# A six-layer cross network on one core: how the first rows come in and the last rows go out

## The chip, the core and the metric

The kernel runs on one core of a Trainium2 chip. TensorE (PE) multiplies matrices and writes PSUM. VectorE (DVE) and ScalarE (ACT) read PSUM and write on-chip memory (SBUF), GpSimd (POOL) computes on SBUF alone, and SyncE (SP) issues transfers. Transfers (DMAs) are issued from the queues of SP, ACT and POOL. The metric is the device time of one execution in microseconds (us). The profile's span is the part of it between the first and the last recorded instruction.

## The reference

```python
B, F, D, L = 4096, 26, 16, 6          # Din = F * D = 416
x = x0                                # (4096, 416), bf16
for l in range(L):                    # ws: (6, 416, 416), bs: (6, 416)
    x = x0 * (x @ ws[l] + bs[l]) + x
```

Written out, x stays x0 times a sum, so the kernel keeps the sum in PSUM: after layer l, PSUM holds the sum over all layers so far of x_l @ ws[l], the bias is the running sum of bs, and x_(l+1) = x0 * (PSUM + bias sum), where that bias sum begins with a one.

## The kernel before

**Layout.** x0 and x are kept transposed: features on partitions, rows along the free dimension. The 416 features are three chunks of 128 (`NC = 3`) and a rest of 32 that is called the tail. The 4096 rows are four super-blocks of 1024 rows (`SB`), each with two halves of 512 (`H`), half A and half B. For each super-block the six layers run one after the other, so there are 24 periods of the same shape.

**One period.** TensorE multiplies half A's three chunks (`chunk(m, 0)`), then the tail's rows (`row`, line 351, and the matmul at line 367), then the tail's columns, then half B's three chunks. All matmuls of weights are cut in tiles of 32 columns (`tile_mm`, line 212), four of which run side by side. VectorE turns each finished PSUM bank into the next x (`scalar_tensor_tensor`, line 459). ScalarE, GpSimd and again ScalarE do the same for the tail (lines 506, 199, 486).

**The start.** The first 768 rows of x0 come as plain rows into `xin_sb`, whose slot j holds rows 128j to 128j+127; TensorE transposes them. Only rows 768 to 1023 and the later super-blocks are transposed by the DMA itself. Line 121 (SP) loads slots 0 and 1, line 474 (ACT) slots 2 and 3, each in one transfer of 208 KB; line 123 loads slots 4 and 5. Between them stand layer 0's weights (`w_sb`, lines 122 and 475), and on ACT the tail's last rows (`xtl_sb`) and two of the four pieces of layer 0's tail weights (`load_wt`, line 107; the two others are issued by POOL). TensorE first multiplies constants (`fill(14)`: 14 rounds of four matmuls with 256 columns), whose result is thrown away, then makes twelve 128x128 transposes (line 250) in the order of `IN_ORDER`, pairs (h, c) of 256-row half and chunk. VectorE copies chunks 0 and 2 of each to `x0T_sb` (line 432), ScalarE chunk 1 (line 481). Layer 0 of half A then runs with k outermost: for each k, it waits for that chunk's copies and multiplies it with all three output chunks. Before k = 2 come the bias sums, the transposes of the tail and those of slots 4 and 5.

**The end.** The last super-block's output is transposed back by TensorE into PSUM and copied to `o_sb`, whose slots are again 128 rows. Half A's chunks are transposed between the matmuls of the last layer and copied by ScalarE (line 527). Half B (slots j0+4 to j0+7) follows at the end: eight transposes of chunks 0 and 1 into PSUM bank 4, then four of chunk 2 into banks 5 and 0 (line 406), and three copies out: VectorE copies chunks 0 and 1 of all four slots in one instruction (line 464), ScalarE chunk 2 of slots j0+4 and j0+5 (line 537), VectorE chunk 2 of slots j0+6 and j0+7 (line 468). SP stores slots j0+6 and j0+7 (line 159), ACT slots j0+4 and j0+5 (line 543).

**Order.** Every engine's program is written out by hand, and each engine runs its own in order; semaphores tie them together. A wait holds back all that stands behind it on the same engine, DMA issues too. `s_xin[h]` counts landed loads of half h, 16 for each transfer; `s_inT` the finished transposes, two at a time; `s_inD` and `s_inA` the copies by VectorE and ScalarE; `s_pB` the output transposes; `s_oeD`, `s_oeA` and `s_oet` the output copies.

Of the kernel before, what the change touches and what calls it, by code (L numbers as in the profile page):

```python
# [8 lines left out]
ACTF = mybir.ActivationFunctionType  # L9


def bass_standalone__dcn_v2_cross__recsys_kernel(
# [8 lines left out]
    NC = 3  # L21
    DF = 128 * NC
# [8 lines left out]
    NL = NS * L  # L31

    with ExitStack() as es:  # L33
# [8 lines left out]
        xin_sb = sb("xin_sb", [128, 6, D])  # L42
# [11 lines left out]
        o_sb = sb("o_sb", [128, NJ, D])  # L54
# [6 lines left out]
        psT = ps.bitcast(BF16)  # L61
# [7 lines left out]
        s_xin = [sem("s_xin%d" % i) for i in range(3)]  # L69
        s_xtl0, s_x4 = sem("s_xtl0"), [sem("s_x4%d" % i) for i in range(NS - 1)]  # L70
        s_w = [sem("s_w%d" % i) for i in range(L)]
        s_wt = [sem("s_wt%d" % i) for i in range(2)]
        s_x0T = [sem("s_x0T%d" % i) for i in range(NS)]
        s_inT, s_inD, s_inA = sem("s_inT"), sem("s_inD"), sem("s_inA")
        s_tp, s_te = sem("s_tp"), sem("s_te")
        s_ti, s_to, s_mb = sem("s_ti"), sem("s_to"), sem("s_mb")
        s_xa, s_xb = sem("s_xa"), sem("s_xb")
# [3 lines left out]
        s_pA, s_pB, s_pt, s_out = sem("s_pA"), sem("s_pB"), sem("s_pt"), sem("s_out")  # L81
        s_oet, s_oeA, s_oeD = sem("s_oet"), sem("s_oeA"), sem("s_oeD")

        x0_v = x0.rearrange("(j p) d -> p j d", p=128)
# [7 lines left out]


        IN_BANKS = ((3, 4, 6), (0, 5, 7))
        IN_ORDER = ((0, 0), (1, 0), (0, 1), (1, 1), (0, 2), (1, 2))
        THIRD = (3, 6, 7)
        HALVES = (slice(0, 64), slice(64, 128))

# [6 lines left out]
        def load_wt(eng, g, a, b, done):  # L105
            n0, n1 = ((0, 256), (256, DF))[g % 2]
            eng.dma_start(
                wt_sb[lane(g), a:b, 0:n1 - n0], ws[a:b, DF:D, n0:n1].rearrange("l p n -> p l n")
            ).then_inc(done, 16)

        @block.sync
        def _(sp):
            def load_rows(s):
                sp.dma_start_transpose(
                    x4_sb[:, s - 1:s, :], x0[s * SB:(s + 1) * SB, D - 128:D]
                ).then_inc(s_x4[s - 1], 16)
                sp.dma_start_transpose(
                    x0T_sb[:, :, s * SB:(s + 1) * SB], x0[s * SB:(s + 1) * SB, 0:DF]
                ).then_inc(s_x0T[s], 16)

            sp.dma_start(xin_sb[:, 0:2, :], x0_v[:, 0:2, :]).then_inc(s_xin[0], 16)
            sp.dma_start(w_sb[:, 0, 0, :], ws[0, 0:128, :]).then_inc(s_w0, 16)
            sp.dma_start(xin_sb[:, 4:6, :], x0_v[:, 4:6, :]).then_inc(s_xin[2], 16)
            sp.dma_start_transpose(x0T_sb[:, :, 768:SB], x0[768:SB, 0:DF]).then_inc(s_x0T[0], 16)
            for l in range(1, L):
                if l > 1:
                    sp.wait_ge(s_ti, (1, 2, 2, 2)[l - 2])
                if l == L - 1:
                    load_rows(1)
                sp.dma_start(w_sb[:, l, :, :], wmain(l)).then_inc(s_w[l], 16)  # L130
                if l == 1:
                    for g in range(4):
                        load_wt(sp, g, 1, L, s_wt[1])
            for s in range(NS - 1):
                n = (s + 1) * L
                sp.wait_ge(s_xa, NC * n)
                sp.wait_ge(s_xb, NC * n)
                for c in range(NC):
                    sp.dma_start_transpose(
                        o_sb[:, s * JS:(s + 1) * JS, c * 128:(c + 1) * 128], xo_sb[:, s, c, :]  # L140
                    ).then_inc(s_oT, 16)
                sp.wait_ge(s_xt, n)
                sp.dma_start_transpose(ot_sb[:, s, :, :], xot_sb[:, s, :]).then_inc(s_ot, 16)
                if s < NS - 2:
                    load_rows(s + 2)
                sp.wait_ge(s_oT, 16 * NC * (s + 1))
                sp.wait_ge(s_otc, s + 1)
                sp.dma_start(
                    out_v[:, s * JS:(s + 1) * JS, :], o_sb[:, s * JS:(s + 1) * JS, :]
                ).then_inc(s_out, 16)  # L150
            j = (NS - 1) * JS
            sp.wait_ge(s_oeA, 2)
            sp.dma_start(out_v[:, j:j + 4, 0:256], o_sb[:, j:j + 4, 0:256]).then_inc(s_out, 16)
            sp.wait_ge(s_oeA, 3)
            sp.wait_ge(s_oet, 1)
            sp.dma_start(out_v[:, j:j + 4, 256:D], o_sb[:, j:j + 4, 256:D]).then_inc(s_out, 16)
            sp.wait_ge(s_oeD, 2)
            sp.wait_ge(s_oet, 1)
            sp.dma_start(out_v[:, j + 6:j + 8, :], o_sb[:, j + 6:j + 8, :]).then_inc(s_out, 16)
            sp.wait_ge(s_out, 16 * (NS + 3))  # L160
# [49 lines left out]
        def _(pe):  # L210
# [8 lines left out]
            def fill(n):  # L219
                for i in range(n):  # L220
                    for q in range(4):
                        tile_mm(ps[lane(q), 7, 0:256], const[:, 0:32], const, q, True)
# [18 lines left out]
                            )  # L241
                    ins.then_inc(s_inT, 1)

            fill(14)
            pe.wait_ge(s_set, 1)
            for i, (h, c) in enumerate(IN_ORDER):
                if i in (0, 1):
                    pe.wait_ge(s_xin[h], 16)
                for j in range(2 * h, 2 * h + 2):
                    ins = pe.transpose(  # L250
                        out=psT[:, IN_BANKS[h][c], (j % 2) * 128:(j % 2 + 1) * 128],
                        in_=xin_sb[:, j, c * 128:(c + 1) * 128], identity=ident[:, :],
                    )
                ins.then_inc(s_inT, 1)
# [20 lines left out]
            for s in range(NS):  # L275
                for l in range(L):
# [25 lines left out]

                    def before_a(k):
                        if n == 0:
                            pe.wait_ge((s_inD, s_inA, s_inD)[k], (2, 2, 4)[k])
                        else:
                            pe.wait_ge(s_xa, NC * (n - 1) + k + 1)
                            if l == 0 and k == 0:
                                pe.wait_ge(s_x0T[s], 16)
# [47 lines left out]
                    for part in range(2):  # L357
# [4 lines left out]
                        for h in range(2):  # L362
                            g, wm = 2 * h, slice(part * 128, part * 128 + 128)
# [10 lines left out]
                        for h in range(2):  # L374
                            g = 2 * h + 1
# [23 lines left out]
            for r in range(2):  # L399
                for q in range(4):  # L400
                    c = r * 128 + 32 * q
# [3 lines left out]
            def out_transposes(c, j, bank, slot):  # L405
                return pe.transpose(
                    out=psT[:, bank, slot * 128:(slot + 1) * 128],
                    in_=xo_sb[:, NS - 1, c, j * 128:(j + 1) * 128], identity=ident[:, :],
                )

            pe.wait_ge(s_xb, NC * NL - 1)
            for jj in range(4):
                for c in range(2):
                    ins = out_transposes(c, 4 + jj, 4, jj * 2 + c)
            ins.then_inc(s_pB, 1)
            pe.wait_ge(s_xb, NC * NL)
            pe.wait_ge(s_oeA, 1)
            for jj in range(4):
                ins = out_transposes(2, 4 + jj, (5, 0)[jj // 2], jj % 2)
                if jj % 2:  # L420
                    ins.then_inc(s_pB, 1)

        j0 = (NS - 1) * JS

        @block.vector
        def _(dve):
# [16 lines left out]
            for s in range(NS):  # L443
                for l in range(L):
                    n = s * L + l
                    for half in range(2):
                        if half == 0:
                            dve.wait_ge(s_ti, n + 1)
                        for c in range(NC):
# [10 lines left out]
                                out=dst, in0=ps[:, NC * half + c, :], scalar=cb_sb[:, c, l:l + 1],  # L460
                                in1=x0T_sb[:, c, o:o + H], op0=ALU.add, op1=ALU.mult,
                            ).then_inc((s_xa, s_xb)[half], 1)
            dve.wait_ge(s_pB, 1)
            dve.tensor_copy(  # L464
                out=o_sb[:, j0 + 4:j0 + 8, 0:256], in_=psT[:, 4, :].rearrange("p (j d) -> p j d", d=256)
            ).then_inc(s_oeD, 1)
            dve.wait_ge(s_pB, 3)
            dve.tensor_copy(
                out=o_sb[:, j0 + 6:j0 + 8, 256:DF], in_=psT[:, 0, 0:256].rearrange("p (j d) -> p j d", d=128)
            ).then_inc(s_oeD, 1)  # L470

        @block.scalar
        def _(act):
            act.dma_start(xin_sb[:, 2:4, :], x0_v[:, 2:4, :]).then_inc(s_xin[1], 16)
            act.dma_start(w_sb[:, 0, 1:NC, :], ws[0, 128:DF, :].rearrange("(k p) n -> p k n", p=128)).then_inc(s_w[0], 16)
            act.dma_start(xtl_sb[:, :, :], x0_v[:, 6:JS, DF:D]).then_inc(s_xtl0, 16)
            for g in (1, 3):
                load_wt(act, g, 0, 1, s_wt[0])
            for h in range(2):
                act.wait_ge(s_inT, h + 3)  # L480
                act.activation(  # L481
                    out=x0T_sb[:, 1, h * 256:(h + 1) * 256], in_=psT[:, IN_BANKS[h][1], 0:256], func=ACTF.Copy
                ).then_inc(s_inA, 1)
# [41 lines left out]
            for c in range(NC):  # L525
# [7 lines left out]
                out=o_sb[:, j0:j0 + JS, DF:D].rearrange("p (g r) f -> p r g f", r=2),  # L533
                in_=ps[:, 3, 0:256].rearrange("p (r g f) -> p r g f", g=4, f=DR), func=ACTF.Copy,
            ).then_inc(s_oet, 1)
            act.wait_ge(s_pB, 2)
            act.activation(
                out=o_sb[:, j0 + 4:j0 + 6, 256:DF], in_=psT[:, 5, 0:256].rearrange("p (j d) -> p j d", d=128), func=ACTF.Copy
            ).then_inc(s_oeA, 1)
            act.wait_ge(s_oet, 1)  # L540
            act.wait_ge(s_oeA, 4)
            act.wait_ge(s_oeD, 1)
            act.dma_start(out_v[:, j0 + 4:j0 + 6, :], o_sb[:, j0 + 4:j0 + 6, :]).then_inc(s_out, 16)


# [26 lines left out]
```

## Time and profile before

| What | Value |
|---|---|
| median of 6 runs | 130.9 us (130.49 to 131.19) |
| the six runs | 131.17, 130.58, 130.63, 131.19, 131.18, 130.49 us |
| profiled execution: its own time, its span | 130.97 us, 129.1 us |
| PE busy | 124.6 us, 97% of the span |
| DVE busy | 100.1 us, 78% |
| ACT busy | 71.3 us, 55% |
| POOL busy | 23.1 us, 18% |
| bytes moved by DMAs | 12.54 MB, 97 GB/s in the mean |

Busy time is counted per engine, and the parts overlap. Of PE it says little on how well it is used: matmuls are pipelined, and one that waits for its turn counts as busy. The start of one instruction against the start of the next is the better measure. "Landing" is the time from the start of a DMA's issue to the arrival of all its data. A chain of waits goes back from the last instruction, at each step to what released it or to the instruction before it on the same engine.

### The profile page before, as it was taken

The numbers are of one execution on the slowest core, as the hardware profiler recorded it, in microseconds if no ns is written. First come the engines' busy times: TensorE is split into PE (matmuls) and PEld (weight loads), VectorE is DVE, ScalarE is ACT, GpSimd is POOL, SyncE is SP. The second block draws the span as 40 slices with busy tenths as digits, with TensorE's granted clock in tenths as the row PEclk, the third lists the DMA queues.
The fourth block names the chain that finished last, engine by engine and source line by source line (L and its number), as shares of the span: only waits on it lengthen the run. The fifth ranks groups of instructions, "written<-read, shape, count | busy, mean of one in ns | idle before, by whom it ended". The sixth has DMA issues, their size and how long they took to land.

```text
span 129.1 us, 5404 instructions
## 1 busy us (share of the span) xinstructions
PE 124.6 (97%) x2448; PEld 62.7 (49%) x2448; DVE 100.1 (78%) x154; ACT 71.3 (55%) x163; POOL 23.1 (18%) x42
## 2 busy tenths in 40 slices
PE   7999999999999999999999999999999999999980
PEld 6654444444444445445445445445445445445450
DVE  2339779779779779779779779779779789789780
ACT  0626457376736456476745456475745555555670
POOL 7802102102102113012012013012022023022130
PEclk9999999999999999999999999999999999999999
DMA  3963299600008699700008996700009900700026
GB/s 105 316 147 104 53 260 162 157 0 5 0 10 161 121 118 199 261 3 5 5 0 164 110 177 149 264 5 0 5 0 76 197 1 0 264 5 5 3 78 191
DMA packets 32918, 12.54 MB, mean 97 GB/s; under 512 B 25338, under 2 KB 32896, under 8 KB 32896
## 3 DMA queue, kind: packets, MB, share of 16 engines
q1 hardware_dynamic: 31488, 11.47, 42.4%
q10 hardware_dynamic: 1184, 0.67, 1.7%
q8 instruction: 19, 0.31, 1.0%
q0 software_dynamic: 224, 0.06, 0.2%
q14 instruction: 3, 0.02, 0.1%
HBM read 2.90 MB, written 3.41 MB: 49 GB/s over the span
## 4 chain that ended last, share of the span: by engine, by line
PE 96%; DVE 1%; DVEq 0%; issue 0%
PE ps L212 84%; PE ps L351 10%; PE ps L250 1%; DVE xo_sb L459 1%; DVE o_sb L464 0%; DVEq L33 0%; PE ps L367 0%
## 5 line engine op out<-in xcount | busy, mean ns | idle before, releaser
L459 DVE SCALAR_TENSOR_TENSOR xT_sb<-ps,cb_sb,x0T_sb 128x512 bf16<-128x512 f32 x120 | 80.9, 743 | 16.4 <-PE ps L351 16.4
L212 PE MATMUL ps<-xT_sb,w_sb 128*32 128x512 bf16 (+1 forms) x1680 | 89.0, 364 | 0.0
L212 PEld LDWEIGHTS ps<-xT_sb,w_sb 128*32 128x32 bf16 x1680 | 43.0, 97 | 38.7 <-issue 4.2
L486 ACT ACTIVATE xt_sb<-xt_sb 32x256 bf16<-32x256 bf16 x80 | 33.1, 414 | 16.6 <-POOL xt_sb L199 15.9
L506 ACT ACTIVATE t_sb<-ps,cb_sb 64x256 f32<-64x256 f32 x48 | 22.5, 468 | 30.1 <-PE ps L212 29.8
L199 POOL TENSOR_TENSOR xt_sb<-t_sb,x0t_sb 128x256 bf16<-128x256 f32 x20 | 13.4, 671 | 83.7 <-ACT t_sb L506 83.7
L212 PE MATMUL ps<-x0T_sb,w_sb 128*32 128x512 bf16 (+1 forms) x336 | 18.8, 369 | 0.0
L459 DVE SCALAR_TENSOR_TENSOR xo_sb<-ps,cb_sb,x0T_sb 128x512 bf16<-128x512 f32 x23 | 15.6, 744 | 3.7 <-PE ps L351 3.3
L212 PEld LDWEIGHTS ps<-x0T_sb,w_sb 128*32 128x32 bf16 x336 | 8.5, 98 | 7.9 <-issue 1.5
L351 PE MATMUL ps<-xt_sb,wt_sb 32*128 32x512 bf16 x80 | 12.1, 379 | 0.0
L519 ACT ACTIVATE x0t_sb<-x_sb 32x256 bf16<-32x256 bf16 x24 | 9.9, 413 | 0.4
L367 PE MATMUL ps<-xt_sb,wt_sb 32*128 32x512 bf16 x40 | 7.8, 385 | 0.0
L351 PE MATMUL ps<-xt_sb,wc_sb 32*128 32x256 bf16 x80 | 7.7, 268 | 0.0
L351 PEld LDWEIGHTS ps<-xt_sb,wt_sb 32*128 32x128 bf16 x80 | 2.3, 92 | 8.5 <-DVE xT_sb L459 8.5
L351 PEld LDWEIGHTS ps<-xt_sb,wc_sb 32*128 32x128 bf16 x80 | 4.0, 93 | 2.3
L199 POOL TENSOR_TENSOR xot_sb<-t_sb,x0t_sb 128x256 bf16<-128x256 f32 x4 | 2.7, 671 | 12.6 <-ACT t_sb L506 12.6
L212 PE MATMUL ps<-const-bfloat16-1.0 128*32 128x256 bf16 x56 | 3.2, 417 | 0.8 <-PEq L557 0.8
L481 ACT ACT_TABLE_LOAD x1 | 1.3, 1283 | 3.6 <-issue 3.6
L432 DVE COPY x0T_sb<-ps 128x256 bf16<-128x256 bf16 x4 | 1.0, 290 | 2.9 <-PE ps L250 2.9
L212 PEld LDWEIGHTS ps<-const-bfloat16-1.0 128*32 128x32 bf16 x56 | 2.3, 142 | 1.2 <-issue 0.8
L351 PE MATMUL ps<-x0t_sb,wt_sb 32*128 32x512 bf16 x16 | 2.4, 379 | 0.0
L168 POOL DMA_DIRECT2D wc_sb<-in_ws_dram x4 | 2.2, 549 | 0.0
(44 smaller groups left out, 28.8 us busy)
## 6 DMA issues: line engine op xcount, KB each, us to landing
out_dram<-o_sb SPq DMA_DIRECT2D x3, 832.0 KB, 4.1
w_sb<-in_ws_dram SPq DMA_DIRECT2D x5, 312.0 KB, 3.4
xin_sb<-in_x_dram SPq DMA_DIRECT2D x2, 208.0 KB, 3.4
out_dram<-o_sb SPq DMA_DIRECT2D x1, 256.0 KB, 2.4
xin_sb<-in_x_dram ACTq DMA_DIRECT2D x1, 208.0 KB, 3.2
w_sb<-in_ws_dram ACTq DMA_DIRECT2D x1, 208.0 KB, 3.6
out_dram<-o_sb SPq DMA_DIRECT2D x1, 208.0 KB, 2.2
out_dram<-o_sb ACTq DMA_DIRECT2D x1, 208.0 KB, 2.7
```

Source lines behind the costliest of these rows:

```text
L168: pool.dma_start(wc_sb[lane(g), a:b, 32 * g:32 * g + 32], ws[a:b, DF:D, DF:D].rearrange("l p n -> p l n")).then_inc(s_wc[i], 16)
L199: pool.tensor_tensor(out=dst, in0=t32_sb[:, n % 2, :], in1=x0t_sb[:, s, 0:G], op=ALU.mult).then_inc(s_xt, 1)
L212: return pe.matmul(dst, lhsT=lhsT, rhs=rhs, start=start, stop=True, skip_group_check=True, tile_position=(0, 32 * q),)
L250: ins = pe.transpose(out=psT[:, IN_BANKS[h][c], (j % 2) * 128:(j % 2 + 1) * 128], in_=xin_sb[:, j, c * 128:(c + 1) * 128], identity=ident[ ...
L351: return pe.matmul(dst, lhsT=lhsT, rhs=srct[lane(g), cols], start=l == 0 and start, stop=True, skip_group_check=True, tile_position=(32 * ...
L367: pe.matmul(ps[:, NC * h + 2, :], lhsT=wt_sb[lane(g), l, 0:128], rhs=srct[lane(g), :].rearrange("p (b r) -> p b r", b=2)[:, ::-1, :], star ...
L432: dve.tensor_copy(out=x0T_sb[:, c, h * 256:(h + 1) * 256], in_=psT[:, IN_BANKS[h][c], 0:256]).then_inc(s_inD, 1)
L459: dve.scalar_tensor_tensor(out=dst, in0=ps[:, NC * half + c, :], scalar=cb_sb[:, c, l:l + 1], in1=x0T_sb[:, c, o:o + H], op0=ALU.add, op1= ...
L481: act.activation(out=x0T_sb[:, 1, h * 256:(h + 1) * 256], in_=psT[:, IN_BANKS[h][1], 0:256], func=ACTF.Copy).then_inc(s_inA, 1)
L486: ins = act.activation(out=buf[lane(g), G:2 * G], in_=buf[lane(g ^ 1), 0:G], func=ACTF.Copy)
L506: ins = act.activation(out=t32_sb[HALVES[h], n % 2, :], in_=tail(h), func=ACTF.Identity, bias=cb_sb[HALVES[h], NC, l:l + 1],)
L519: ins = act.activation(out=x0t_sb[lane(g), s + 1, swap * G:(swap + 1) * G], in_=x4_sb[96:128, s, r * G:(r + 1) * G], func=ACTF.Copy,)
```

## The change

At the start, each of the four 128-row slots 0 to 3 gets a transfer of its own: SP issues slots 0 and 2, ACT slots 1 and 3. TensorE now waits for two transfers for each half (32 counts in place of 16), transposes all of half 0 ahead of half 1, and runs 11 rounds of filler instead of 14. The wait counts of the copies follow: with the new order, the first matmul's two chunk-0 copies are VectorE's first and third. Of the two pieces of tail weights that ACT issued, one moves to SP, ahead of slots 4 and 5, and the other stays on ACT, between its two copies.

At the end, the eight transposes of chunks 0 and 1 go chunk by chunk, chunk 0 into bank 4 and chunk 1 into bank 1, with a count after each. ScalarE copies chunk 0 (512 elements per partition), VectorE chunk 1 (512). Of chunk 2, ScalarE copies slot j0+4 (128) and VectorE the other three (384). TensorE waits for two of ScalarE's earlier copies ahead of the eight transposes, since bank 1 is reused, and the stores wait for one copy more.

```diff
-        IN_ORDER = ((0, 0), (1, 0), (0, 1), (1, 1), (0, 2), (1, 2))
+        IN_ORDER = ((0, 0), (0, 1), (0, 2), (1, 0), (1, 1), (1, 2))
...
-            sp.dma_start(xin_sb[:, 0:2, :], x0_v[:, 0:2, :]).then_inc(s_xin[0], 16)
+            for j in (0, 2):
+                sp.dma_start(xin_sb[:, j, :], x0_v[:, j, :]).then_inc(s_xin[j // 2], 16)
             sp.dma_start(w_sb[:, 0, 0, :], ws[0, 0:128, :]).then_inc(s_w0, 16)
+            load_wt(sp, 1, 0, 1, s_wt[0])
             sp.dma_start(xin_sb[:, 4:6, :], x0_v[:, 4:6, :]).then_inc(s_xin[2], 16)
...
             sp.wait_ge(s_oeD, 2)
+            sp.wait_ge(s_oeA, 4)
             sp.wait_ge(s_oet, 1)
...
-            fill(14)
+            fill(11)
             pe.wait_ge(s_set, 1)
             for i, (h, c) in enumerate(IN_ORDER):
-                if i in (0, 1):
-                    pe.wait_ge(s_xin[h], 16)
+                if c == 0:
+                    pe.wait_ge(s_xin[h], 32)
...
                         if n == 0:
-                            pe.wait_ge((s_inD, s_inA, s_inD)[k], (2, 2, 4)[k])
+                            pe.wait_ge((s_inD, s_inA, s_inD)[k], (3, 2, 4)[k])
...
             pe.wait_ge(s_xb, NC * NL - 1)
+            pe.wait_ge(s_oeA, 2)
+            for c in range(2):
+                for jj in range(4):
+                    ins = out_transposes(c, 4 + jj, (4, 1)[c], jj)
+                ins.then_inc(s_pB, 1)
+            pe.wait_ge(s_xb, NC * NL)
             for jj in range(4):
-                for c in range(2):
-                    ins = out_transposes(c, 4 + jj, 4, jj * 2 + c)
-            ins.then_inc(s_pB, 1)
-            pe.wait_ge(s_xb, NC * NL)
-            pe.wait_ge(s_oeA, 1)
-            for jj in range(4):
-                ins = out_transposes(2, 4 + jj, (5, 0)[jj // 2], jj % 2)
-                if jj % 2:
+                ins = out_transposes(2, 4 + jj, 0 if jj else 5, jj)
+                if jj in (0, 3):
                     ins.then_inc(s_pB, 1)
...
-            dve.wait_ge(s_pB, 1)
+            dve.wait_ge(s_pB, 2)
             dve.tensor_copy(
-                out=o_sb[:, j0 + 4:j0 + 8, 0:256], in_=psT[:, 4, :].rearrange("p (j d) -> p j d", d=256)
+                out=o_sb[:, j0 + 4:j0 + 8, 128:256], in_=psT[:, 1, 0:512].rearrange("p (j d) -> p j d", d=128)
             ).then_inc(s_oeD, 1)
-            dve.wait_ge(s_pB, 3)
+            dve.wait_ge(s_pB, 4)
             dve.tensor_copy(
-                out=o_sb[:, j0 + 6:j0 + 8, 256:DF], in_=psT[:, 0, 0:256].rearrange("p (j d) -> p j d", d=128)
+                out=o_sb[:, j0 + 5:j0 + 8, 256:DF], in_=psT[:, 0, 128:512].rearrange("p (j d) -> p j d", d=128)
             ).then_inc(s_oeD, 1)
...
-            act.dma_start(xin_sb[:, 2:4, :], x0_v[:, 2:4, :]).then_inc(s_xin[1], 16)
+            for j in (1, 3):
+                act.dma_start(xin_sb[:, j, :], x0_v[:, j, :]).then_inc(s_xin[j // 2], 16)
...
-            for g in (1, 3):
-                load_wt(act, g, 0, 1, s_wt[0])
             for h in range(2):
-                act.wait_ge(s_inT, h + 3)
+                if h == 1:
+                    load_wt(act, 3, 0, 1, s_wt[0])
+                act.wait_ge(s_inT, NC * h + 2)
...
-            act.wait_ge(s_pB, 2)
+            act.wait_ge(s_pB, 1)
             act.activation(
-                out=o_sb[:, j0 + 4:j0 + 6, 256:DF], in_=psT[:, 5, 0:256].rearrange("p (j d) -> p j d", d=128), func=ACTF.Copy
+                out=o_sb[:, j0 + 4:j0 + 8, 0:128], in_=psT[:, 4, 0:512].rearrange("p (j d) -> p j d", d=128), func=ACTF.Copy
             ).then_inc(s_oeA, 1)
+            act.wait_ge(s_pB, 3)
+            act.activation(out=o_sb[:, j0 + 4, 256:DF], in_=psT[:, 5, 0:128], func=ACTF.Copy).then_inc(s_oeA, 1)
             act.wait_ge(s_oet, 1)
-            act.wait_ge(s_oeA, 4)
-            act.wait_ge(s_oeD, 1)
+            act.wait_ge(s_oeA, 5)
+            act.wait_ge(s_oeD, 2)
```

## The prediction

> **What bounds the kernel now.** I read the page first, then the chain of work that ended last in order of time, because the change touches only the first 9 us and the last 6. From 9.2 to 121 us that chain is TensorE and nothing else (84% of the span line 212, 10% line 351), in periods of 4.87 us which the change leaves alone. Its two ends, start and length in us:
>
> ```profile
> 0.85 3.18 PE ps L212 x46
> 4.03 1.39 PE ps L250 x12
> 5.42 3.27 PE ps L212 x89
> ...
> 124.44 0.75 DVE xo_sb L459
> 125.19 0.60 DVE o_sb L464
> 125.79 0.20 DVEq L33
> ```
>
> At the start the filler matmuls run until the first transposes, and TensorE hardly pauses: what sets the start of the transposes (3.96) is the end of the filler, not the data. The landings of the transfers concerned (issue windows 0.8 to 1.3 and 2.9 to 3.2; KB, then us from issue to landing) show it:
>
> ```profile
> xin_sb<-in_x_dram SPq DMA_DIRECT2D x1, 208.0 KB, 2.9
> xin_sb<-in_x_dram ACTq DMA_DIRECT2D x1, 208.0 KB, 3.2
> wt_sb<-in_ws_dram ACTq DMA_DIRECT2D x1, 8.0 KB, 4.4
> ```
>
> Issued at 0.81 and 0.82, rows 0 to 255 are there at 3.71 and rows 256 to 511 at 4.02; the first transpose starts at 3.96 and the third, which needs the second half, at 4.15. Neither waits.
>
> The second thing to see is TensorE's own speed, by line (min/median/max ns, then first and last start):
>
> ```profile
> L212 PE MATMUL ps<-const-bfloat16-1.0 x56: 373/418/421, 0.8 to 3.6; 128*32 128x256 bf16 x56
> L250 PE MATMUL ps<-ident,xin_sb x12: 287/314/314, 4.0 to 5.1; 128*128 128x128 bf16 x12
> L212 PE MATMUL ps<-x0T_sb,w_sb x8: 547/579/609, 5.4 to 5.8; 128*32 128x512 bf16 x8
> L212 PE MATMUL ps<-x0T_sb,w_sb x20: 379/379/551, 5.8 to 6.8; 128*32 128x512 bf16 x20
> L406 PE MATMUL ps<-ident,xo_sb x12: 219/219/230, 124.4 to 125.4; 128*128 128x128 bf16 x12
> ```
>
> The same 128x128 transpose takes 314 ns at 4 us and 219 at 124; the 512-column matmul falls from 579 to 379 at about 6.1 us. In the timeline, transposes follow each other by 0.107 us at the start (0.056 at the end), groups of four 512-column matmuls by 0.40 us until 6.1 and by 0.217 after. So everything before 6.1 us runs at half speed, though the page's clock row shows 9 from the first slice.
>
> At the end (timeline, start and length):
>
> ```profile
> 125.11 0.68 DVE L464 COPY o_sb<-ps 128x1024 bf16<-128x1024 bf16 x1
> 125.25 0.40 PE L406 MATMUL ps<-ident,xo_sb 128*128 128x128 bf16 x4 [0.20 <-DVE xo_sb L459]
> 125.57 0.38 ACT L537 ACTIVATE o_sb<-ps 128x256 bf16<-128x256 bf16 x1 [0.64 <-PE ps L406]
> 125.71 0.28 DVE L468 COPY o_sb<-ps 128x256 bf16<-128x256 bf16 x1
> 126.02 0.37 SPq L159 DMA_DIRECT2D out_dram<-o_sb  x1
> 126.03 0.46 ACTq L543 DMA_DIRECT2D out_dram<-o_sb  x1
> ```
>
> The last chunk leaves VectorE at 125.19, its four transposes end at 125.65, the small copies at 125.96 and 125.99, then two stores go out together; ACT's lands 2.7 us later, SP's 2.2. The big copy (0.68) ends at 125.79 and holds VectorE's last copy back by only 0.02: that could have started at about 125.69, 0.04 after the last transpose.
>
> [...]
>
> **The change, part by part.**
>
> *Loads.* Each 208 KB load becomes two of 104 KB, one per queue, so rows 0 to 255 come first on both queues. By 3.0 us some 258 KB had moved (4 GB/s for 2 us, 250 for 1), so 416 KB were through at about 3.43, and the second half landed at 4.02, 0.6 later. 208 KB are through at about 2.8; with the same lag they land at 3.4 (3.15 to 3.6 as ends: no queueing at all; or ACT's first transfer as late against SP's as now, 0.3). The second half lands where it does now, about 4.0: the same bytes are ahead of it.
>
> *Filler.* 14 rounds in 3.18 us are 0.213 to 0.227 each; three fewer end it 0.64 earlier, at 3.32. The data is then later than the filler: transposes start at about 3.46 (3.32 to 3.68) instead of 3.96. TensorE gets a hole of 0.15 to 0.35 us that it does not have now.
>
> *Order of the transposes.* Six of the first half, 0.64 us, reach to 4.10; the second half is there. All twelve (1.28) end streaming at 4.75, and the first matmul follows 0.13 later, as now (5.21 to 5.35): 4.88. Its new wait is for the third VectorE copy, of the eighth transpose: start 3.46 + 0.75, + 0.31 length + 0.04 = 4.56, + 0.29 copy = 4.85, + 0.06 to TensorE = 4.91. With its queue position it is 4.95 against 5.35: 0.40 earlier. Behind this wait stand all matmuls; its w_sb row block (landed at 4.33 now, same bytes ahead) is there.
>
> *What 0.40 is worth.* [...] Work done before 6.1 is done at half speed, so 0.40 us more of it saves 0.20. By groups: three at 4.95, 5.37, 5.80, the fourth from 6.17, then 0.217 each, ending at 6.82 instead of 7.00. Gain 0.19, and all of the 112 us after it shift by this.
>
> *Other DMAs moved.* SP issues two more ahead of the third load, the transpose and layer 1's weights, each 0.45 to 0.5: these go out 1.0 later (2.8, 3.3, 4.6). The third load now lands at 5.63 and is needed at 7.3; the transpose at 7.10, needed at 9.16; layer 1's weights at 8.29, needed at 11.45, its tail weights at about 9.7, needed at 13.5. A full 1.0 fits in each gap even with the gap 0.2 shorter (0.66 left at the least). ACT's loads of weights and tail rows go out 0.5 later (4.95 and 5.97 now, needed at 6.14 and 7.1); they stand behind the same bytes, so cost nothing unless the whole 0.5 shows and then still fit. ACT's table load starts at 2.9 instead of 3.64, so its first copy can start at 4.2 instead of 4.93. Its remaining tail-weight load (line 107) is issued between its copies, at 4.2 to 4.7; the second copy then ends by 5.5, needed at 6.17. That load lands at 4.2 + 2.5 to 4.4 = 6.7 to 8.6; the rows that need it are due at 8.43. I take 7.2: now it stands behind 224 KB on its queue, then behind nothing. Cost nothing, at worst 0.2.
>
> *The tail.* ScalarE now copies chunk 0 of the last half (512 elements, 0.60 by line 527) from 124.87 to 125.47, VectorE chunk 1 (512: between 0.28 for 256 and 0.68 for 1024, 0.41) from 125.11 to 125.52. Both then wait for the last chunk's transposes: ScalarE for the first (128 elements, 0.28 by its slope of 0.21 per 256), ending at 125.79; VectorE for all four, at 125.69, with three blocks instead of two: 384 elements, 0.35, ending at 126.03 against 125.99. Both stores need it, also ACT's, which now need only ScalarE's at 125.96: they issue at about 126.07 and 126.09. Cost 0.05; ends 0 (if the copy is no longer than two blocks) and 0.1. TensorE's new wait for ScalarE's second copy (ended 124.1, needed 124.43) is past.
>
> *Sum.* 129.1 - 0.19 + 0.05 = 128.96 of span, 130.97 (that execution's own time) - 0.14 = 130.83. That execution lies 0.07 above the median of the six runs, so 130.75 on their scale.
>
> **The rivals.**
>
> *The start counts in full.* If the clock's release moves with the work, or if in unprofiled runs TensorE waits for the rows (the six runs lie in two groups, 130.5 to 130.6 and 131.2, so something at the start or end varies by 0.6), the gain is 0.40 to 0.6: 130.9 - 0.5 + 0.05 = 130.45. Against: the release at 6.1 is in the middle of even work.
>
> [...]
>
> *ACT's late tail-weight load.* Should it take the 4.4 of now or more, TensorE waits at 8.43 ahead of the first rows: 0.2 at 4.4, 0.8 at 5.0, so 130.95 to 131.55.
>
> *The split does nothing*, if ACT's first rows come as late as SP's two loads together now (3.7): transposes at 3.78, gain 0.06, 130.9. It is within the first case's range.
>
> **How the numbers follow.** Sum as worked out: 0.44, its own range 130.4 to 131.0. In full: 0.26, 130.2 to 130.6. [...] Late tail weights: 0.12. 0.3% is 0.39 us, about what a measurement of this kernel can tell from no change: under 130.51 is faster, over 131.29 slower. Of the first, 0.15 is faster, 0.27 same, 0.02 slower; the second faster; the third slower; of the fourth 0.08 slower, 0.04 same. Together 0.41, 0.31, 0.28. The range 130.2 to 131.5 leaves out the late clock and a little at the low end, under 0.2.
>
> **What would show it.** First transpose near 3.46 with a hole before it, and first w_sb matmul near 4.95; 512-column matmuls still falling to 379 ns at about 6.1; bias matmuls at 6.9 instead of 7.10; the period unchanged at 4.87; last copy 384 wide ending 0.04 later relative to the last chunk. A fall to 379 ns only after 9 us means the second rival; a wait ahead of line 351 at 8.4 the third.

## The result, and the profile after

The median of 33 runs is 131.5 us (130.61 to 133.27), against 130.68 for 68 runs of the kernel before (130.28 to 131.47). The ratio is 1.0048, 95% interval 1.0033 to 1.0063: slower by about half a per cent, where the prediction had faster (130.75). The runs lie in two groups, 17 from 130.61 to 131.50 (median 131.26) and 16 from 132.29 to 133.27 (median 132.70); the median of all is just the highest run of the lower group. The ratio, which leaves out what is far above a kernel's fastest runs, understates the loss: no run of before is above 132, so here the upper group belongs to the change, and the experiments show where it comes from. The profiled execution took 131.15 us (130.97 before), span 129.3 (129.1).

First, for the kernel after, the chain of work that ended last, in order of time (start and length, us):

```profile
0.81 0.41 SPq L122
1.28 0.42 SPq L122
1.74 3.75 DMA w_sb<-in_ws_dram
5.54 3.04 PE ps L215 x92
8.75 0.37 PE ps L354
...
124.57 0.76 DVE xo_sb L462
125.38 0.41 PE ps L409 x4
125.81 0.36 DVE o_sb L471
```

Before, the chain began on TensorE with the filler. Now it begins on SP: two row transfers are issued one after the other, then the weights, and TensorE's first weight matmul starts when those have landed. The timeline of TensorE (in brackets the idle time before an instruction, and what ended it) has the two pauses:

```profile
0.85 2.54 PE L215 MATMUL ps<-const-bfloat16-1.0 128*32 128x256 bf16 x44 [0.85 <-PEq L563]
3.57 1.11 PE L253 MATMUL ps<-ident,xin_sb 128*128 128x128 bf16 x12 [0.18 <-DMA xin_sb<-in_x_dram]
5.54 1.52 PE L215 MATMUL ps<-x0T_sb,w_sb 128*32 128x512 bf16 x24 [0.86 <-DMA w_sb<-in_ws_dram]
...
8.72 0.09 PEld L354 LDWEIGHTS ps<-x0t_sb,wt_sb 32*128 32x128 bf16 x1 [0.64 <-DVE x0T_sb L444]
```

The transposes start at 3.57, 0.39 earlier than before, after a pause. The first weight matmul starts at 5.54, not at 4.95 as predicted and 0.19 later than before (5.35), after 0.86 us of waiting. (The last bracket names a copy of VectorE. The one of its two copies that the tail's rows wait for had ended at 8.18; what came last was ACT's tail weights, at 8.50.) The landings of what was issued from 0.5 to 2.5 us (KB, then us from issue to landing):

```profile
xin_sb<-in_x_dram SPq DMA_DIRECT2D x2, 104.0 KB, 2.5
xin_sb<-in_x_dram ACTq DMA_DIRECT2D x2, 104.0 KB, 2.5
w_sb<-in_ws_dram ACTq DMA_DIRECT2D x1, 208.0 KB, 4.4
w_sb<-in_ws_dram SPq DMA_DIRECT2D x1, 104.0 KB, 3.8
```

Before, the second of the weight transfers read (issued from 1.3 to 1.8):

```profile
w_sb<-in_ws_dram SPq DMA_DIRECT2D x1, 104.0 KB, 3.0
```

SP's weights (line 122 before, 123 now) go out at 1.74 instead of 1.32 and take 3.8 us instead of 3.0, so they land at 5.50 instead of 4.33. What they stand behind is the same 416 KB. The stretches of half a microsecond show the transfers themselves (after the length of the stretch comes PE's busy time; the last two columns are the mean busy share of the DMA engines and GB/s). Before:

```profile
3.00:3.50 0.50, 0.50 (x16) 0.43 (x12) 0.00 (x0) 0.00 (x0) 0.50 (x2) 1.00 1.11 365
3.50:4.00 0.50, 0.50 (x13) 0.09 (x6) 0.00 (x0) 0.36 (x1) 0.50 (x2) 1.00 1.11 371
4.00:4.50 0.50, 0.50 (x9) 0.50 (x7) 0.11 (x1) 0.50 (x1) 0.50 (x2) 1.00 1.09 339
```

After:

```profile
3.00:3.50 0.50, 0.39 (x8) 0.00 (x0) 0.00 (x0) 0.50 (x1) 0.50 (x2) 1.00 0.95 228
3.50:4.00 0.50, 0.43 (x5) 0.46 (x6) 0.02 (x1) 0.50 (x1) 0.50 (x2) 1.00 0.61 135
4.00:4.50 0.50, 0.50 (x10) 0.40 (x7) 0.49 (x3) 0.38 (x2) 0.50 (x2) 1.00 0.93 231
```

From 3 to 4.5 us the DMA engines move 135 to 231 GB/s in place of 339 to 371. By the stretches from 1.5 us on, 452 KB have moved by 3.5 us, little more than the rows' 416, and 635 by 4.5 (795 before): of the 728 KB of rows and weights, at least 93 are still to come. The semaphore of the weights goes up in 16 steps, and each is here taken as the landing of one share of the transfer: the first is at 3.89 and the last at 5.50; before, all sixteen were between 4.04 and 4.33.

TensorE's speed, by tile (min/median/max ns, then first and last start):

```profile
L253 PE MATMUL ps<-ident,xin_sb x12: 219/224/314, 3.6 to 4.5; 128*128 128x128 bf16 x12
L215 PE MATMUL ps<-x0T_sb,w_sb x24: 379/379/392, 5.5 to 6.7; 128*32 128x512 bf16 x24
```

In this execution half speed ended at 3.98 in place of 6.09 (there the trace's record of the granted clock begins, with 1.0): the later transposes take 219 ns in place of 314, and no weight matmul takes the 579 of before. So this profile shows a mild case. Its sum closes: first weight matmul +0.19; early full speed -0.30 (bias matmuls at 6.99 against 7.10); ahead of the tail's rows +0.24 (8.75 against 8.62), since the tail weights landed at 8.50; end +0.05. Together +0.18, and the execution is 131.15 - 130.97 = 0.18 longer.

The end of the kernel after in the timeline:

```profile
125.24 0.41 DVE L467 COPY o_sb<-ps 128x512 bf16<-128x512 bf16 x1
125.38 0.40 PE L409 MATMUL ps<-ident,xo_sb 128*128 128x128 bf16 x4 [0.20 <-DVE xo_sb L462]
125.64 0.28 ACT L545 ACTIVATE o_sb<-ps 128x128 bf16<-128x128 bf16 x1
125.81 0.36 DVE L471 COPY o_sb<-ps 128x384 bf16<-128x384 bf16 x1 [0.16 <-PE ps L409]
126.20 0.37 SPq L162 DMA_DIRECT2D out_dram<-o_sb  x1
126.28 0.42 ACTq L549 DMA_DIRECT2D out_dram<-o_sb  x1
```

The 384-wide copy is now last. From the last chunk's departure from VectorE (125.32) to the end of the span it takes 3.96 us, where it was 3.91.

### The profile page after: what moved, and what is told of

The parts are those of the page before. It is cut to its first block, busy times and chain, and to the rows that moved or that the text cites. A ratio compares the mean times of both kernels' runs of the same rounds, so it can differ in the third digit from the quotient of the medians.

```text
span 129.3 us, 5383 instructions
## 1 busy us (share of the span) xinstructions
PE 123.5 (96%) x2436; PEld 61.7 (48%) x2436; DVE 100.0 (77%) x154; ACT 71.9 (56%) x164; POOL 23.2 (18%) x42
## 4 chain that ended last, share of the span: by engine, by line
PE 92%; DMA 3%; DVE 1%; SPq 1%; issue 0%
PE ps L215 82%; PE ps L354 10%; DMA w_sb<-in_ws_dram 3%; SPq L122 1%; DVE xo_sb L462 1%; PE ps L409 0%; DVE o_sb L471 0%; PE ps L370 0%
## 5 line engine op out<-in xcount | busy, mean ns | idle before, releaser
L215 PE MATMUL ps<-const-bfloat16-1.0 128*32 128x256 bf16 x44 | 2.5, 417 | 0.8 <-PEq L563 0.8
```

The lines of the kernel that those rows point to most:

```text
L215: return pe.matmul(dst, lhsT=lhsT, rhs=rhs, start=start, stop=True, skip_group_check=True, tile_position=(0, 32 * q),)
```

## The experiments

"Over 132" counts runs above 132 us. The kernel before had none in any batch; its medians were 130.65 (40 runs), 130.78 (68), 130.79 (67), 130.78 (19) and 130.63 (19). Where a diff is against the kernel after, it says so.

### Which end of the kernel, and is it the split

**The new start with the old end, and the old start with the new end.** Each is one half of the change's diff on the kernel before.

> The changed start with the end of before. If the loss sits in the start (layer 0's weights land later and TensorE waits for them ahead of its first weight matmul): about 0.5 us slower than before in most runs, first weight matmul at 5.3 or later, and part of the runs another 1.5 us slower, as with the whole change. If the loss sits in the end: within 0.2 us of before.

> The start of before with the changed end. If the start is to blame: 0.05 to 0.15 us slower than before, and no run far from the others. If the end is to blame: about 0.6 us slower.

New start: 131.31 us, 3 of 11 over 132, ratio 1.0051 (1.0028 to 1.0074). New end: 130.82, none of 14 over 132, 1.0014 (1.0000 to 1.0028), with 3.96 us from the last chunk to the end. The loss and the upper group are in the start. The profiled execution of the new start took 132.37 us and so shows the upper group from inside. Its timeline of TensorE:

```profile
3.56 0.80 PE L252 MATMUL ps<-ident,xin_sb 128*128 128x128 bf16 x6 [0.17 <-DMA xin_sb<-in_x_dram]
4.54 0.82 PE L252 MATMUL ps<-ident,xin_sb 128*128 128x128 bf16 x6 [0.18 <-DMA xin_sb<-in_x_dram]
5.54 2.75 PE L214 MATMUL ps<-x0T_sb,w_sb 128*32 128x512 bf16 x24 [0.18 <-DMA w_sb<-in_ws_dram]
...
10.06 0.38 PE L353 MATMUL ps<-x0t_sb,wt_sb 32*128 32x512 bf16 x1
```

The first weight matmul is at 5.54, as in the kernel after. But the series of 24 takes 2.75 us in place of 1.52: half speed lasts until 9.13, and the tail's rows come at 10.06 in place of 8.75. That is 1.3 us lost after the weights had arrived.

**The whole change, but with the rows in two transfers of 208 KB.** Diff against the kernel after (each half again waits for 16):

```diff
-            for j in (0, 2):
-                sp.dma_start(xin_sb[:, j, :], x0_v[:, j, :]).then_inc(s_xin[j // 2], 16)
+            sp.dma_start(xin_sb[:, 0:2, :], x0_v[:, 0:2, :]).then_inc(s_xin[0], 16)
...
-            for j in (1, 3):
-                act.dma_start(xin_sb[:, j, :], x0_v[:, j, :]).then_inc(s_xin[j // 2], 16)
+            act.dma_start(xin_sb[:, 2:4, :], x0_v[:, 2:4, :]).then_inc(s_xin[1], 16)
```

> The whole change, but rows 0 to 255 and 256 to 511 again come in one transfer each, from SP and ACT. If the four small transfers spread the DMA engines and so delay layer 0's weights: these land by 4.5 and the first weight matmul starts at about 5.2, after transposes that start at 3.8. If it is not the split but the one DMA more that is issued ahead of them, the weights still come in time here, since nothing more stands ahead of them than in before: both give about 130.8. If the clock is what counts (the hole ahead of the transposes): the hole is longer here, 0.5 us, and the kernel as slow as the changed one or slower, 131.3.

**The split alone**, on the kernel before: the same edit the other way round (each half waits for 32), and nothing else of the change.

> The kernel before, but with the four 128-row transfers (and the wait for two of them); order of the transposes, filler, tail weights and end as before. If the number of transfers alone delays layer 0's weights: the first weight rows land at about 5.4 instead of 4.3 to 4.6, and the kernel is 0.3 us or more slower than before, with runs near 132.5. If it takes the whole new start (the moved tail weights, the shorter filler) to do the harm: within 0.2 us of before.

Unsplit: 130.88, none of 22 over 132, 1.0011 (0.9995 to 1.0027); the weights land at 4.44 and the first weight matmul is at 5.34. Split alone: 131.6, 3 of 15 over 132, 1.0075 (1.0048 to 1.0102); they land at 5.79 and TensorE waits 1.04 us for them. (Some 0.17 of its loss came later by its profile: POOL's loads `wc_sb`, at 9.10 there and 8.14 before, held back the second part of the tail's rows.) The split alone carries the loss; the new order, the shorter filler and the moved tail weights don't.

### Number of transfers, or lateness of the issue

**Weights second on SP.** Against the kernel after, SP issues them between its two row transfers.

```diff
-            for j in (0, 2):
-                sp.dma_start(xin_sb[:, j, :], x0_v[:, j, :]).then_inc(s_xin[j // 2], 16)
+            sp.dma_start(xin_sb[:, 0, :], x0_v[:, 0, :]).then_inc(s_xin[0], 16)
             sp.dma_start(w_sb[:, 0, 0, :], ws[0, 0:128, :]).then_inc(s_w0, 16)
+            sp.dma_start(xin_sb[:, 2, :], x0_v[:, 2, :]).then_inc(s_xin[1], 16)
```

> The whole change, but SP issues layer 0's first weight rows between its two row transfers instead of behind them. If the late weights cost the time: they land by 4.4, the first weight matmul starts at about 5.0, and the kernel is 0.4 to 0.6 us faster than the changed one, near before or a little better (130.5 to 130.8). If the clock or the tail is to blame: as the changed one, 131.3.

132.72, 4 of 6 over 132, 1.0132 (1.0091 to 1.0174): the expected gain did not come. The weights land in time (4.21), but now rows 256 to 511, issued third, land at 5.43, and the first weight matmul is at 6.35. What goes out third on SP is late, whichever transfer it is.

**Two transfers, late weights.** The unsplit kernel with a wait for one of VectorE's clearings ahead of both weight transfers, which go out at 1.89:

```diff
+            sp.wait_ge(s_zero, 2)
             sp.dma_start(w_sb[:, 0, 0, :], ws[0, 0:128, :]).then_inc(s_w0, 16)
...
+            act.wait_ge(s_zero, 2)
```

> The whole change with the rows in two transfers, as in unsplit, but SP and ACT hold layer 0's weights back until VectorE's second memset (about 1.87 us), so that they are issued as late as in the changed kernel, without a transfer more. If it is the later issue that delays the weights: they land at 5.0 or later, 0.5 us slower than unsplit, and some runs near 132.5. If it is the number of transfers ahead of them: they land by 4.7, and the time is that of unsplit, 130.9.

131.5, 9 of 22 over 132, 1.0068 (1.0042 to 1.0094). The weights land at 5.46, and the slow stretch of the transfers is back though the rows come in two transfers:

```profile
3.50:4.00 0.50, 0.19 (x3) 0.22 (x4) 0.00 (x0) 0.50 (x1) 0.50 (x2) 1.00 1.11 148
```

Lateness of the issue is enough. Three theories of why so little lateness (0.42 us) costs 1.17 us of landing were tried.

*The bias load of POOL slips in front of the weights.* Bias load behind the weights, in the kernel after (first; diff) and in the one with two transfers and late weights (second); bias load ahead of POOL's first memset in the kernel before (third):

```diff
-            pool.dma_start(bsa_sb[1:L + 1, :], bs[:, :]).then_inc(s_bs, 16)
...
+            pool.wait_ge(s_zero, 2)
+            pool.dma_start(bsa_sb[1:L + 1, :], bs[:, :]).then_inc(s_bs, 16)
```

> The whole change, but POOL issues its small load of the biases at 1.9 us or later instead of 1.38, so that it is behind layer 0's weights (1.74) again, as it is in before (1.38 against 1.32). If this load, once ahead of the weights, is what makes them straggle: its first packets come after 3.6, the weights land by 4.7, the first weight matmul starts at about 5.0, and the kernel takes 130.4 to 130.8 without runs near 132.7. If it is only that the weights are issued later: they still land after 5.2, and the time is that of the changed kernel, 131.3 and 132.7.

> As unsplit_late (rows in two transfers, weights held back to 1.87 us), with the load of the biases behind the weights, at 1.9 or later. If the order against the biases counts: weights land by 4.8, time that of unsplit, 130.9. If the issue time counts: after 5.2, with runs near 132.7, as unsplit_late.

> The kernel before, but POOL issues the load of the biases first of all (0.8 us), ahead of the weights at 1.32. If a POOL load ahead of the weights makes them straggle: they land after 5.0 instead of 4.3 to 4.6, the kernel is 0.4 us or more slower, with runs near 132.5. If the issue time of the weights is what counts: nothing changes, within 0.2 us of before.

Refuted by the first two: the weights still land at 5.61 and 5.65, and 7 of 14 and 7 of 22 runs are over 132 (132.07 us, 1.0026, 0.9997 to 1.0055; 131.05, 1.0033, 1.0010 to 1.0057). The third doesn't test it: POOL's first issue could not be earlier than 1.35, where it was 1.38, and the weights landed at 4.21. It came out at 131.14, 1.0035 (1.0021 to 1.0049), with 1 of 22 over 132; a later landing of POOL's later loads (`wc_sb` at 8.82 against 8.14) is the only difference seen: the second part of the tail's rows, which needs them, comes 0.47 us after the first in place of 0.23. It was not tested further.

*The transfers queued behind the weights slow them*: two transfers and late weights, and behind the weights on SP and on ACT a wait for the first transposes (`wait_ge(s_inT, 1)`). *The landing grows with the lateness*: the wait ahead of the weights is for one count of `s_zero` in place of two, so that they go out at 1.47, in two batches; the 1.89 was repeated beside the second.

> As unsplit_late, but what is issued behind the weights on both queues (a piece of tail weights and rows 512 to 767 on SP, the tail's last rows on ACT) is held back until the first transposes are done, about 4.2 us. If the transfers queued behind the weights slow these, the first weight rows land by 4.8. If the late issue alone does: after 5.2 all the same. The held transfers then come late themselves, so the time is not compared, only the landing.

> As unsplit_late, but the weights are held back only to VectorE's first memset, about 1.5 us (unsplit 1.32, unsplit_late 1.89). [...] the landing of the first weight rows lies between the two (4.44 and 5.46), at 4.6 to 5.0. If something blocks all that is issued after a certain moment: it is at one of the two values, 4.5 or 5.4.

> The unsplit start with the weights' issue held to about 1.47, as once before (then 130.6 us, none of 14 runs over 132, weights landed at 5.42 in the profile). If the landing at 5.42 was a rarity, this profile shows the first weight rows by 4.7, the first weight matmul at 5.35, a median near that of before (within 0.2 us) and no run over 132. If a late landing is the rule here and does not by itself make the slow group, they land at 5.3 or later again and still no run is over 132. If it is the rule and does make the slow group, 4 in 10 runs are over 132 this time.

> The unsplit start with the weights' issue held to 1.89, as once before (then 131.5 us, 9 of 22 runs over 132, weights landed at 5.46). If the group over 132 belongs to the kernel and not to the chip of that batch, about 4 in 10 runs are over 132 again, the median is near 131.5 and the weights land at 5.3 or later; if it belonged to the chip, none is over 132 and the median is near 130.9.

With nothing behind them, the weights issued at 1.90 still land at 5.34 (131.76, 4 runs, none over 132, 1.0081, 1.0051 to 1.0111). Transfers behind them aren't the cause. Its time says less, since its later loads are late as well (tail's rows at 9.37). Issued at 1.47 they landed at 5.42 in one profiled execution and at 4.81 in the other, and the runs are those of before: 130.6 (14 runs; 0.9993, 0.9975 to 1.0010) and 130.69 (14; 1.0004, 0.9988 to 1.0020), none over 132. So the last landing varies from execution to execution at 1.47, and in the traces was never before 5.3 from 1.74 on. The steps of the semaphore show more than the last landing. At 1.47, 15 of the 16 shares of SP's weights were in by 4.30 in the first profile and 14 in the second: the 5.42 was one straggler. At 1.28 to 1.32 (five profiles) it was 15 or 16, at 1.74 to 1.90 (eleven profiles) at most 6. So the change comes between 1.47 and 1.74. The repeat at 1.89, on the chip of the second 1.47: 132.6 (6 runs, one far off at 185.5; ratio 1.0134, 1.0091 to 1.0177), three over 132 at 132.6 to 133.1, landing 5.47. Here the same chip has the upper group for one kernel and not for the other, so it belongs to the kernel. Why so many shares come late from 1.74 on isn't settled.

### The upper group

**A filler in the second pause**, to ask whether the pause makes the upper group: after the loop of transposes of the kernel after (`fill` takes the bank as a second argument, since bank 7 is in use by then):

```diff
                 ins.then_inc(s_inT, 1)
+            fill(3, 2)
```

> The whole change, with three more rounds of filler (into PSUM bank 2, before it is first used) between the transposes and the first weight matmul, where TensorE now waits for the weights. The weights land as late as in the changed kernel. If the runs near 132.7 are those [...]: they are gone or rare here, all runs between 130.6 and 131.8, median about 131.3. If they have another cause (a slow transfer, say): half of the runs are still near 132.7.

131.22, 1 of 22 over 132, 1.0031 (1.0020 to 1.0042). Its timeline of TensorE:

```profile
3.56 1.44 PE L253 MATMUL ps<-ident,xin_sb 128*128 128x128 bf16 x12 [0.17 <-DMA xin_sb<-in_x_dram]
4.92 0.83 PE L215 MATMUL ps<-const-bfloat16-1.0 128*32 128x256 bf16 x12
5.74 1.87 PE L215 MATMUL ps<-x0T_sb,w_sb 128*32 128x512 bf16 x24
```

The weights are as late as ever (5.70) and the first weight matmul is later than in the kernel after (5.74), yet the upper group is nearly gone (16 of 33 before this edit). Work whose result is thrown away helps here by filling the pause. That speaks for the upper group being full speed that comes late, and for the pause making it late. The profiles of the other kernels agree: of the 18 executions profiled, the three above 132 us (new start with old end, 132.37; weights second, 132.51; bias load late, 132.94) came to full speed at 9.13, 8.38 and 10.27, and none of the others later than 7.40. No execution of the kernel after that lies in its upper group was itself profiled. What is left with the filler, 0.3%, fits the late first weight matmul (5.74 against 5.35) and the end (0.05); the tail weights were in time in this trace (8.43, the rows at 9.06).

### The tail weights, and a best version

**ACT's tail-weight load ahead of its two copies**, against the kernel after:

```diff
+            load_wt(act, 3, 0, 1, s_wt[0])
             for h in range(2):
-                if h == 1:
-                    load_wt(act, 3, 0, 1, s_wt[0])
```

> The whole change, but ACT issues its one load of tail weights ahead of its two copies instead of between them. In the changed kernel that load landed at 8.50 and TensorE's first tail rows started at 8.75. If this load holds TensorE back: here it lands before 7.5, and where the clock is released early the tail rows start about 0.2 us sooner after layer 0's last k step; the median falls by 0.1 to 0.2 us. If not, nothing changes.

131.19, 6 of 22 over 132, 1.0017 (0.9999 to 1.0035). The load lands at 7.18 instead of 8.50. Its timeline around the tail's rows:

```profile
7.99 0.83 PE L215 MATMUL ps<-x0T_sb,w_sb 128*32 128x512 bf16 x12
...
8.75 0.38 PE L354 MATMUL ps<-x0t_sb,wt_sb 32*128 32x512 bf16 x1
```

From the third group of weight matmuls to the rows it is 0.76 us, as before the change (7.86 to 8.62); in the kernel after it was 1.00 (7.75 to 8.75). The gain of 0.24 in the trace is clear; in the ratio it is within the uncertainty. It is there only when full speed comes early: in the traces where it came at 6.58 or later (the one with the filler is among them), the tail weights landed before the rows were due.

**New start, early tail weights, late bias, old end**, the edits shown put together:

> What the runs so far speak for, together: the new start with the four transfers, the tail weights issued ahead of ScalarE's copies, the biases behind the weights, and the end of before. If the order against the biases is the cause: first weight matmul at about 4.95, no wait for tail weights, about 0.2 us faster than before (130.4 to 130.5). If not: as start_only, 131.3.

131.38, 9 of 22 over 132, 1.0038 (1.0013 to 1.0062); weights at 6.04. It doesn't beat the kernel before, and none of the versions does.

## Why the prediction was wrong

**Rows, transposes, filler: right.** Rows 0 to 255 landed at 3.43 (3.4 predicted), the first transpose was at 3.57 (3.46; 3.32 to 3.68), and the second half landed at 4.13 (4.0). The start of the transfers was not as assumed from the profile before: from 2 to 3 us the four small transfers moved 315 KB, the two large ones 250.

**The step that failed: "its w_sb row block (landed at 4.33 now, same bytes ahead) is there".** Counting bytes ahead assumed that a transfer issued later is still waiting when its turn comes. In its place the runs show that the time of the issue counts: with the same 416 KB ahead, SP's weights issued at 1.32 landed between 4.21 and 4.58, and issued at 1.74, behind one more issue of 0.42 us on the same queue, between 5.49 and 6.04; issued at 1.89 or 1.90 with no transfer more they landed between 5.34 and 5.65. That the rows' bytes then run out before the weights' are ready is argued from the dip to 135 GB/s; why they are ready so late stays open. The prediction counted such delays for the transfers further down (1.0 us there), and here trusted the bytes. The same holds of ACT's weights, said to "stand behind the same bytes" and given at most 0.5: they landed at 6.18, 1.24 later than before (4.94), though TensorE waited only some 0.03 us for them.

**First weight matmul.** 5.54 instead of 4.95: where a start 0.40 earlier was to gain 0.19, it came 0.19 later. That the profiled execution lost no more than 0.18 in all is luck: full speed came early (3.98) and gave back 0.30.

**The second rival, full speed late (the "late clock" of the range): right, and given too little.** Given 0.18, with a fall to 379 ns only after 9 us as its sign, it came in 16 of 33 runs, 1.44 us above the others (132.70 - 131.26), if all of the upper group is late full speed; in the three profiles above 132 us it came at 8.38 to 10.27. The prediction counted a hole of 0.15 to 0.35 us ahead of the transposes, where TensorE waits 0.18 for the rows; the wait for the weights, 0.86, comes on top. The fall "at about 6.1", as a fixed time, was wrong too: the same kind of start came to full speed anywhere from 3.47 to 10.27 in the profiles. The prediction fixed that time by one profile; what sets it isn't shown.

**The start counts in full: no.** The time of full speed does move, but not with the work: with transposes from 3.57 and 3.56 and the first weight matmul at 5.54 in both, it came at 3.98 in the kernel after and at 9.13 in the new start with the old end.

**ACT's late tail weights: right as a rival.** It took 4.3 us to land (8.50), and cost 0.24, close to the 0.2 given for 4.4.

**The tail: right**, 0.05 in the trace.

**The range** ended at 131.5, the median measured. That is chance, since the median is only the top of the lower group; the range left out the upper one. The chances held 0.28 for slower, spread over mechanisms that had each been seen; what was missing was the late landing of the layer's first weights, which lengthened the pause (0.86 us) and so made late full speed likely (16 of 33 runs, if the upper group is that).

## What to carry to other kernels

Splitting a load puts an issue (0.41 to 0.46 us here) ahead of everything that stands behind it on its queue; at a start, check when the next transfer goes out, and not only how many bytes are ahead of it. A pause of TensorE near the start can cost much more than its length: here, with 0.86 us of waiting for weights, 16 of 33 runs took 1.44 us more than the others, and with that pause filled 1 of 22 was over 132. Full speed came anywhere from 3.47 to 10.27 us in the profiles, so price a pause from several of them, not from one. Where a kernel's runs fall in two groups, look for the profile that lies in the upper one.

## What the runs showed of the hardware

**Pauses and the upper group.** TensorE's idle time from 3 to 5.5 us in one profiled execution (what PE's busy time leaves of five stretches of half a microsecond), and the kernel's runs over 132 us:

| Kernel | Idle, us | Over 132 |
|---|---|---|
| before | 0.00 | 0 of 68 |
| before, bias load first on POOL | 0.00 | 1 of 22 |
| filler in the second pause | 0.16 | 1 of 22 |
| weights at 1.47, second profile | 0.40 | 0 of 14 |
| new start, old end (132.37 us) | 0.49 | 3 of 11 |
| rows in two transfers | 0.51 | 0 of 22 |
| weights at 1.47, first profile | 0.65 | 0 of 14 |
| two transfers, late weights | 0.67 | 9 of 22 |
| bias load behind the weights (132.94 us) | 0.67 | 7 of 14 |
| best version | 0.67 | 9 of 22 |
| split alone | 0.73 | 3 of 15 |
| two transfers, late weights, repeated | 0.83 | 3 of 6, one more at 185.5 |
| two transfers, late weights, late bias | 0.92 | 7 of 22 |
| tail weights ahead of the copies | 0.97 | 6 of 22 |
| after | 1.00 | 16 of 33 |

The kernels with the most idle time have an upper group, those with the least have none or one run of 22. Between them the order fails (0.49 with 3 of 11, 0.65 with none of 14). One execution stands for each kernel, and one that comes to full speed early has shorter transposes and so more idle time. How much of a pause it takes isn't shown.

**What the time of full speed is worth with no change at all.** Executions whose weights were in time or nearly so, by the time of full speed and their own: 5.56, 130.57 us (weights at 1.47, second profile); 6.09, 130.97 (before); 7.00, 131.49 (weights at 1.47, first); 7.11, 131.47 (rows in two transfers). That is 0.90 us over 1.55 us of half speed more. An estimate from the spacing of the groups of four matmuls in before (0.40 us at half speed, 0.217 after) gives half speed 0.71 of it; the first weight matmul, at 5.23 in the first of them against 5.34 to 5.46, gives 0.11 to 0.23. It is enough for the 0.7 us by which the six runs of before scatter (130.49 to 131.19), though none of those six is profiled (the profile of before is of another execution).

**Sixteen shares that don't land together.** A transfer of 104 KB landed within 0.3 us from its first share to its last when issued at 1.32 (before), and over 1.6 us when issued at 1.74 (after), with the first share no later (4.04 and 3.89).
